# Stage-1 tables in two pieces, smaller first loads of the kernel rows, and an early SiLU table, in a fused long-convolution and MLP kernel

## The chip, the cores and the metric

The kernel runs on one core of a Trainium2 chip. Its time is the device time of one execution in microseconds (us). Eleven executions are known: 180.72 to 186.76, median 183.02. One more was taken with the hardware profiler; it took 181.62, and its trace is the source of every duration below.

The engines: TensorE (PE, with its weight loads, PEld, shown apart), VectorE (DVE), ScalarE (ACT), GpSimd (POOL) and SyncE (SP). SP and POOL issue the DMA transfers here, and ACT issues three small ones at the start.

## The reference

Sequence S = 2048, width D = 640, inner width F = 1728, one batch, bfloat16.

```
xn = layernorm(x)
kv = causal_shift_conv4(k, shift_k) * v
y  = irfft(rfft(pad(kv)) * rfft(pad(ssm_k)))[:S] + kv * ssm_D     # convolution over the sequence
s  = xn * y
g  = silu(gelu(xn @ w1 + b1) @ w2 + b2)
out = x + s * g
```

## The kernel before

**Two halves of work.** The MLP (xn @ w1, gelu, @ w2, silu) is the larger part of TensorE's work. The convolution is done as a two-stage transform written as matmuls with sine and cosine tables. The 640 channels are cut into two blocks b of H = 320 columns; the 2048 tokens lie as 128 partitions by NJ = 16 rows j.

**The convolution's path.** Stage 1 (op kinds `s1k` for the kernel `kT`, `s1u` for the product `kv`; matmuls at L641) multiplies each token row j with the table `W[:, j, :]`. A unit covers 1024 columns in two halves, numbered 2i and 2i+1, so `s1k4` and `s1k5` are one unit. A half is 512 columns of block b's 16 x 320, so `s1k4` reads rows j = 6 and 7, `s1k8` reads j = 12 to 14. Each half takes a pair of the 8 PSUM banks, is evicted by ACT or DVE (`s1ev`, all evictions have line L268) into one of **three staging slots** (two in the tile `mm`, one in the tile `G`), and the unit is stored to DRAM (`s1st`, L646, issued by SP or POOL) as `scrK` or `scrU`. Stage 2 reads the transposed form back (`kin`, `uin`, L750), multiplies (`s2k`, `s2u`, L767), evicts (`s2ev`), forms complex products on DVE (`prod`, `comb`), transforms back (`i1`, L799; it takes two pairs of banks), evicts (`i1ev`) and stores (`cst`, L810, to `scrC`). At the end `cin` (L841) reads it back, `i2` (L821) makes the result and `ym` (L828, DVE) multiplies it into `xn`; `fin` (L555, L561) adds x and `store` writes out. There are 12 conv units (6 for each b). `uin` rotates over four slots, so unit u+4 is loaded after `cst` of unit u has landed.

**The MLP's path.** `xt` transposes xn on PE (L492), `xtev` evicts; `f1h` and `f1` are the first matmuls (L507; `f1h` is half a column group), `f1p` the last rows of two groups (L538), then `gelu` (L513), `f2` (L588), `silu` (L592) and `f2m` (L595, halves at L601).

**The tables.** On DVE `iq0`, `iq1`, `iq2` (L453, L456, L458) make the angles for all 16 rows in one 128x1024 instruction each; two ACT `wsin` (L462, L464) turn them into the sine and cosine halves of `W`. All of `W` is one buffer, so the first stage-1 matmul waits for the second `wsin`. `tabsin` (L443) makes the small stage-2 tables with Silu first, to have the table set that holds both Silu and Sin. `wbm` and `wbev` (L472) spread the shift weights over the partitions, and `kv` units (L664 to L671, DVE) use them. `warm` (L315) are ten matmuls of zeros. `presin` (L306) is one Silu of one element per partition.

**The order.** Ops, dependencies and candidate engines are declared in the code, but the order, the engine of each op and the PSUM and staging slots come from a written table, `ORDER`: each word names the next op, its engine and its slots. Each engine runs its ops in that order; SP and POOL issue DMAs in that order too, so a DMA whose data is late holds the later ones of its queue. In the version before, PE runs all fillers, then `s1k8 s1k4 s1k9`, then the first `f1h`; ACT starts with table load, evictions, table load, `wsin`.

Of the kernel before, what the change touches and what calls it, by code (L numbers as in the profile page):

```python
# [11 lines left out]
I32 = mybir.dt.int32  # L12
# [25 lines left out]
NB = 512  # L38
NS1 = NJ * H // NB // 2
# [98 lines left out]
2d 4p0 7g 5s 1s -19d 20s -5a 46p0 1a -3p1 -9d 1d 4p2 -24d 32p3 -46g 15d 24a -52p4 31d 1d -22g 19g -23p0 -1p2 -2p0 1p2  # L138
44d 8a -23g 16a -41p0 -7p1 52p0 -18a -5d 44p10 -40d -35p2 8p4 43a 26p2 -39d -1d 24a -22d 1g 15d -37s 7s -2s 53a -52s
-5s 1s 58d 103p60 -10p41 -158d 29d -21s 162p0 -81p20 80a 2a -143d 40p3 -2p6 24p7 -23a 6d 86a -90d 3d 19p0 4p 4a -90s  # L140
21g 1d 39d 37p1 1a -15p 10p3 1a 49p42 -82d 46p6 -67s -37s 61d 80a -36a -24p 66p0 -5p4 45d 1d -29s -121s 60p3 -13a 63a
-86g 1d 2d 14p6 70s -50a -11p7 55a 46d -106p 6a -50s 45a 66p00 2p4 -1a -64a 5p3 -28d 4p21 85a -86d -1d 27a -47s 144d
-154d 64p7 -26p6 117d -116d -6a 129d -126p0 -2p1 1d 25p4 96d -91a 98d 1d 1d 1d 7d -6d 7d 1d 1d 1d 7d -147a -25s 87p21
9s -8a -96s 57a 40p6 -35p5 84s 190d -329s -28a 119a 76d -29s 149d -228p00 14p1 -2p4 3a 100d 1d 1d -93p2 1a -17p3 1a
1p1 23s -15p2 -5a -16a 4a 53p62 2p4 -37a 38a -31p3 243d -241a -89s 329d -262p0 -4p2 25a 202d -174a -44a -4a 80p41 2p6
1a -68p3 1a 65a -84p0 1a 43s -32p1 -81s 82a 41g 51p60 1a 1p4 -91p0 -17a 224d -115a -91a 70s 101p10 2p2 -1a 2a -97p62
2p4 1a 17d -204d 316d -110p01 77p31 2p2 32d 1g -295s 176s 8a -2d 3p4 76a -68d -31a 101a 33d -37d -71p00 111d -300s
335d -144p6 74d -78a 231s1 -223d -5a 61p30 -85g 170d -144a 74p21 -78s 232p4 -224d 105a -49a -129p02 130p3 45a -31a
-70d 1d 101a -94d 132g 1d -214a 69s 75p2 -266s -43s 295a 165s0 -220d 7d 49d 166a -296p6 75p01 102s0 1s -101p4 67a -62d
132a -69d 1p30 2p2 32s 131s0 -310a 75a -74s 76a 219p6 4p0 -154a 2a 149a 5p4 9s1 -10a 2a -221d 1d 1d 132a -126d 124d  # L150
-64p31 2p2 -1a 64a -137s 75a 145d1 -296p60 1a 146d -145p0 1a 294d -121s 126d 1d -214d 64p30 151p46 -150a -64d 125s1 3s
88a -151p2 155p0 2p6 -7a -300p42 86d 61d 6p31 153a -305a 86d 7d -95s 90p01 122s 97a 3p4 -157a 159p6 -1a -224d 2d 224a
-159p3 -4a 158d1 -209p00 -9p4 211s -300p6 154a 17p20 16p3 23s 109s1 -220a -9a -89a 171a 136d -217s 222d 1d 1p04 -313s
91d 227s0 17s0 -21a -128a 3p6 -97d 118p70 10p2 -127d 1d 96a -95d 116a 25p3 79d 1g -215p01 120a -118p6 134a -9p2 -124a
-6p4 140a -9a -155p62 28d -26p0 23d 113p3 -135a 259s2 -261d 138a 106p4 2p0 1a -2d 3d1 -144p2 1a 145p6 2p0 -3d 4a -2a
11p4 -164p3 1a 13p2 -109g 260d 15s2 -165a 166s3 -254s 239p0 -10d 14p6 2p4 1d -2a -4a -126p3 18p2 -17a -214p62 2p4
368s1 -41d -225s 128a -229a -2d 353p0 -14d2 15a -122p3 97p64 -326s 328a -1d -97a -5p2 117d 1d 9p0 4p4 2p6 -5a -16d
30s1 -10a -3d0 5a 1d -182p3 1a 150s -112p0 1a -32p1 1a 157p46 1a 10d 6d -135a -13p0 133d -132a 164s0 1s0 -203p1 1a
185p42 1d -144p0 145a -17s -127a 148p6 2p2 10p4 -232d 233d -10a -2a 3d1 -200p1 1a 209p2 4p6 2p4 -200p0 195d 4a 9s2
-23d -266p1 282a -281d 103p6 -22a 176g -153a 186p2 -1s2 -254d 256a -25p40 1a -272p7 1a 272a 8d2 -214p6 220d -5d -219p2  # L160
225d -220a 229p4 4p0 -237a 234d 13s1 -8p6 -1a -184p3 156s 15p40 -170a 12p21 160a 13d 8s3 17s0 1s1 -40a -158a 167d0 6d
8p6 2p0 4p4 -19d 16a -183p3 187d -6d -180a 172d -14s 29p4 10p0 -9a 10a -196p20 181d1 -180a -2d 183d 5d 10p6 14s2 -13a
-27p40 1a 27d2 13s0 -39a -171p2 199p6 2p4 10p0 -9a 42s0 -44d -199a 171s 14d 41s1 -15a 42s1 -246p31 220s2 -15p6 4p4 2p0
-16d 36s2 -230a 195d -194p2 239s3 -247d 212a 6a -2a -20d -11p60 -176a 178a -166p30 165a 2s -166a 205p4 1a -25p06 10d0
1d 5d 1d -15d -343p2 -4p3 371p4 1d 1d1 -221d 222d -28a -345d 4a 358p06 2a -200p2 199a -198a 1d 208p46 2d -1a 9p0 1d
-38s 39p2 10p4 1d -230d 231d -230p61 219d 2p0 5p4 -708a 483a 3d -30p70 223s 30d -5d -9p2 -2p4 12p0 -9d -2d -3g 34s0
-267p6 1a 247d 20p2 4p4 4s1 -277a 257d 13d -243p0 244d -12s2 19p6 4p2 -254a 246d -271d 257p4 -246p00 265d -21s -228d
-14p1 267d 3s3 -271a 260d 9d -12s -255a 247p6 23p2 -26d 1d 1s 30p4 -37s 24d 5s -4s -272p01 2p1 277d -12s -11d 29d 3d
1s -288a 256d 1s 28d 1s -278d 273d -279a 280s -279d 276d 1s
# [3 lines left out]
def kernel(  # L173
# [87 lines left out]
    def eng(e):  # L261
        return nc.vector if e == "DVE" else nc.gpsimd
# [4 lines left out]
    def evict(e, out_, in_):  # L267
        (nc.scalar.copy if e == "ACT" else nc.vector.tensor_copy)(out=out_, in_=in_)  # L268
# [22 lines left out]
    tok_b, m_b, q_b, a_b, W_b, G_b, tab_b = (Buf() for _ in range(7))  # L291
# [5 lines left out]
    m_v = mm[:, 4 * D:4 * D + 2 * 1024].bitcast(I32)  # L297
    a_v = mm[:, 8 * D:8 * D + 2 * 1024].bitcast(I32)
# [7 lines left out]
    op("presin", "ACT", lambda e: nc.scalar.activation(out=acs[:, CH - 1, 0:1], in_=bias_h[:], func=ACT.Silu), reads=[bias_b])  # L306
# [21 lines left out]
    def load(fn, kb, **kw):  # L328
        return op("load", "SP", fn, size=int(kb * 1024), **kw)
# [32 lines left out]
    for b in range(2):  # L362
        for i in range(2):
            load(lambda e, b=b, i=i: nc.sync.dma_start(out=kT[:, b, 8 * i:8 * i + 8, :], in_=kT_v[:, b, 8 * i:8 * i + 8, :]), 640,
                 writes=kT_b[b][8 * i:8 * i + 8], after=firsts[-1:])
# [76 lines left out]
    def tabsin(e):  # L442
# [10 lines left out]
    op("iq0", "DVE", lambda e: eng(e).tensor_tensor(  # L453
        out=m_v.rearrange("p (a b) -> p a b", a=NJ), in0=tok[:, :, None].to_broadcast([P, NJ, N1]),
        in1=k4[:, None, :].to_broadcast([P, NJ, N1]), op=ALU.mult), reads=[tok_b], writes=[m_b])
    op("iq1", "DVE", lambda e: nc.vector.tensor_scalar(out=m_v, in0=m_v, scalar1=19, scalar2=19, op0=ALU.logical_shift_left,  # L456
                                                       op1=ALU.arith_shift_right), writes=[m_b])
    op("iq2", "DVE", lambda e: nc.vector.scalar_tensor_tensor(out=a_v, in0=m_v, scalar=-1.0, in1=m_v, op0=ALU.mult, op1=ALU.min),  # L458
       reads=[m_b], writes=[a_b])
    W_c = W[:].rearrange("p j (k c) -> p c (j k)", c=2)  # L460
    sc = 2.0 * math.pi / L
    op("wsin", "ACT", lambda e: nc.scalar.activation(out=W_c[:, 1, :], in_=m_v, func=ACT.Sin, scale=-sc * (1.0 - EPS)),  # L462
       reads=[m_b, bias_b], mods=[W_b])
    op("wsin", "ACT", lambda e: nc.scalar.activation(out=W_c[:, 0, :], in_=a_v, func=ACT.Sin, scale=sc, bias=bias_h[:]),  # L464
       reads=[a_b, bias_b], mods=[W_b])
    tmp_hold = [m_b, a_b]
# [3 lines left out]
    for i in range(5):  # L470
        ps = bank()
        op("wbm", "PE", lambda e, ps=ps, i=i: nc.tensor.matmul(out=ps.v[:], lhsT=xtra[0:1, 1024:1024 + P], rhs=wrow_f[:, i * 512:(i + 1) * 512],  # L472
                                                              start=True, stop=True), reads=[wr_b, z_b], writes=[ps])
        op("wbev", "ACT|DVE", lambda e, ps=ps, i=i: evict(e, wb_f[:, i * 512:(i + 1) * 512], ps.v[:]), reads=[ps], writes=[wb_b[i]])
# [150 lines left out]
    def s1_unit(src, src_b, scr, scr_b, i, kind, b):  # L625
        o = Buf(pool=stg_pool, parts=2)
        stages.append(o)
        for t in range(2):
            ps = pair()
            base = NB * (2 * i + t)  # L630
            segs, c = [], base
            while c < base + NB:
                z = min(base + NB, (c // H + 1) * H)
                segs.append((c // H, c % H, z - c, c - base))
                c = z

            def mms(e, segs=segs, ps=ps):
                for j, c, n, at in segs:
                    for h in range(2):
                        r = slice(64 * h, 64 * h + 64)  # L640
                        nc.tensor.matmul(out=ps.v[:, h, at:at + n], lhsT=W[r, j, :], rhs=src[r, b, j, c:c + n], start=True, stop=True)  # L641
# [53 lines left out]
    for i in range(CH):  # L695
# [7 lines left out]
        op("gtr", "PE", gtr, reads=[W_b, id_b], writes=[ps], extra=[u for o in stages for u in o.users])  # L703
# [200 lines left out]
```

## Time and profile before

| what | us |
|---|---|
| median of 11 executions | 183.02 |
| the profiled execution | 181.62 |
| its span, first to last instruction | 179.8 |
| outside the span | 1.82 |
| busy: PE, DVE, ACT, POOL | 169.4, 165.2, 147.0, 17.9 |
| first stage-1 matmul starts | 10.79 |
| last instruction of PE ends | 175.20 |

The profiled execution is 1.40 below the median, so a sum made against it is moved by 1.40 to be compared with the median. A busy share is an average over stages. What counts in a stage is which engine has no idle time, and what ended the idle time of the others. A group's mean is the duration of one instruction; consecutive ACT or DVE instructions overlap a little, so the start-to-start distance in the timeline is the better price of one in a row. For PE the distance between starts is the price: a unit of `f1` takes 1.10, `f1h` 0.55, `f2` 2.0, a stage-1 half 0.28, an `s2` 0.26, `i1` 0.54.

### The profile page before, as it was taken

To read this page: it belongs to the slowest core of one execution; us is meant where nothing else is said; L and a number is where in the kernel's file an instruction comes from. 1 tells how busy PE (TensorE), PEld (TensorE's weight loads), DVE (VectorE), ACT (ScalarE), POOL (GpSimd) and SP (SyncE) were. 2 spreads that over 40 slices of the span, in tenths; PEclk is the share of its full clock that TensorE was granted. 3 is DMA by queue.
4 is the path that set the end of the run, shared out by engine and by line. 5 is a ranking of instruction groups with operands and counts; after the bars stand their busy time and mean duration, and the time that the engine had idled before them with its cause. 6 is when DMAs were issued, how large, how long until landed. Compare 5 with 4: busy or idle time off the path is not lost.

```text
span 179.8 us, 4833 instructions
## 1 busy us (share of the span) xinstructions
PE 169.4 (94%) x1971; PEld 93.0 (52%) x1971; DVE 165.2 (92%) x296; ACT 147.0 (82%) x207; POOL 17.9 (10%) x31
## 2 busy tenths in 40 slices
PE   5979999999999999999999999999999999988990
PEld 1346555444566666656444434344465655654660
DVE  7998989999999999998999969999999999966993
ACT  4999999999998989989999999999899998111110
POOL 7440400001004500000002000010000000100000
PEclk9999999999999999999999999999999999999999
DMA  5999999999696899999298997879896999659284
GB/s 141 378 411 410 359 320 319 422 419 411 228 325 232 288 348 175 360 292 246 90 322 225 295 367 243 248 226 302 240 310 204 288 298 342 187 171 401 106 315 178
DMA packets 42025, 51.43 MB, mean 286 GB/s; under 512 B 7170, under 2 KB 31123, under 8 KB 42004
## 3 DMA queue, kind: packets, MB, share of 16 engines
q1 hardware_dynamic: 41104, 48.41, 84.1%
q0 software_dynamic: 752, 2.72, 4.3%
q8 instruction: 15, 0.25, 0.6%
q10 hardware_dynamic: 148, 0.01, 0.1%
q14 instruction: 6, 0.05, 0.1%
HBM read 31.47 MB, written 18.35 MB: 277 GB/s over the span
## 4 chain that ended last, share of the span: by engine, by line
PE 62%; DMA 19%; DVE 9%; ACT 7%; issue 2%; POOLq 0%; DVEq 0%; SPq 0%
PE ps L507 24%; PE ps L588 23%; DMA scrC<-v_all 7%; PE ps L641 6%; DMA scrU<-G 4%; PE ps L767 4%; DMA v_all<-scrU 3%; DVE xn L828 3%; DMA mm<-scrC 3%; PE ps L799 2%; DVE x L555 2%; ACT v_all L268 2%; DVE G L268 1%; DVE kT L555 1%; PE ps L538 1%
## 5 line engine op out<-in xcount | busy, mean ns | idle before, releaser
L588 PE MATMUL ps<-w_sb,hT 128*128 128x320 bf16 x432 | 63.4, 300 | 0.0
L507 PE MATMUL ps<-xnT,w_sb 128*128 128x512 bf16 (+1 forms) x280 | 61.0, 365 | 0.0
L588 PEld LDWEIGHTS <-hT 128*128 128x128 bf16 x448 | 41.9, 98 | 21.2 <-issue 5.7
L507 PEld LDWEIGHTS <-w_sb 128*128 128x128 bf16 x280 | 25.4, 98 | 28.2 <-issue 5.2
L513 ACT ACTIVATE hT<-ps,b_f 128x512 bf16<-128x512 f32 (+1 forms) x56 | 36.8, 697 | 1.5 <-PE ps L507 0.8
L592 ACT ACTIVATE sl<-ps 128x320 bf16<-128x320 f32 x32 | 14.0, 442 | 22.2 <-PE ps L588 16.7
L268 ACT CAST v_all<-ps 128x960 bf16<-128x960 f32 (+2 forms) x35 | 31.1, 911 | 1.1 <-PE ps L799 0.6
L268 ACT CAST mm<-ps 128x1024 bf16<-128x1024 f32 (+1 forms) x27 | 25.0, 957 | 0.3 <-PE ps L472 0.2
L828 DVE TENSOR_TENSOR xn<-ps,xn 128x640 bf16<-128x640 f32 x16 | 12.6, 815 | 2.8 <-PE ps L821 2.8
L268 ACT CAST G<-ps 128x1024 bf16<-128x1024 f32 x12 | 12.2, 1015 | 0.6 <-DMA scrU<-G 0.4
L667 DVE TENSOR_TENSOR mm<-k_all,mm 128x2560 bf16<-128x2560 bf16 x8 | 11.9, 1490 | 0.2
L664 DVE TENSOR_TENSOR mm<-k_all,mm 128x2560 bf16<-128x2560 bf16 x8 | 11.9, 1487 | 0.1
L268 DVE CAST v_all<-ps 128x960 bf16<-128x960 f32 (+2 forms) x11 | 11.5, 1061 | 0.5 <-ACT hT L513 0.3
L767 PEld LDWEIGHTS <-tabs 64*32 64x32 bf16 x704 | 7.6, 90 | 7.0 <-issue 6.0
L268 ACT CAST k_all<-ps 128x960 bf16<-128x960 f32 x11 | 10.6, 961 | 0.8 <-PE ps L767 0.7
L810 POOL DMA_DIRECT2D scrC<-v_all x3 | 2.5, 818 | 86.6 <-DMA scrC<-v_all 34.0
L395 POOL TENSOR_TENSOR rstd<-veps,mhalf 128x4 f32<-128x4 f32 (+2 forms) x6 | 8.6, 1440 | 24.3 <-DVE veps L393 24.3
L641 PEld LDWEIGHTS <-W 64*128 64x128 bf16 x192 | 6.5, 94 | 8.1 <-issue 5.9
L780 DVE TENSOR_TENSOR k_all<-v_all,k_all 128x960 bf16<-128x960 bf16 x16 | 9.7, 649 | 0.0
L780 DVE TENSOR_TENSOR k_all<-v_all,xtra 128x960 bf16<-128x960 bf16 (+1 forms) x16 | 9.1, 608 | 0.2
L767 PE MATMUL ps<-v_all,tabs 64*32 64x240 bf16 (+1 forms) x352 | 8.5, 262 | 0.4 <-DMA v_all<-scrU 0.3
L641 PE MATMUL ps<-kT,W 64*128 64x320 bf16 (+4 forms) x96 | 6.8, 254 | 1.1 <-ACT W L464 0.9
(104 smaller groups left out, 206.2 us busy)
## 6 DMA issues: line engine op xcount, KB each, us to landing
mm<-scrC SPq DMA_DIRECT2D x8, 640.0 KB, 5.6
v_all<-scrU SPq DMA_DIRECT2D x10, 480.0 KB, 4.3
scrU<-mm SPq DMA_DIRECT2D x8, 512.0 KB, 3.4
scrC<-v_all SPq DMA_DIRECT2D x8, 480.0 KB, 4.5
k_all<-scrK SPq DMA_DIRECT2D x7, 480.0 KB, 5.2
kT<-in_kT_dram SPq DMA_DIRECT2D x4, 640.0 KB, 6.3
scrK<-mm SPq DMA_DIRECT2D x5, 512.0 KB, 5.5
v_all<-in_v_dram SPq DMA_DIRECT2D x4, 640.0 KB, 7.6
```

Of the source, the lines that this page charges most:

```text
L268: (nc.scalar.copy if e == "ACT" else nc.vector.tensor_copy)(out=out_, in_=in_)
L395: pows.append(op("pow", "POOL", lambda e: nc.gpsimd.tensor_tensor(out=rstd[:, a:b], in0=veps[:, a:b], in1=mhalf[:, 0:b - a], op=ALU.pow), ...
L507: nc.tensor.matmul(out=ps.v[:, lo * P:hi * P], lhsT=w1_sb[:, ft, t, :], rhs=xnT_b[c].v[:, t, lo * P:hi * P], start=(t == 0), stop=(t == DT ...
L513: op("gelu", "ACT", lambda e: nc.scalar.activation(out=hT_b[c].v[a:z, ft, :], in_=ps.v[a:z, :], func=ACT.Gelu_apprx_tanh, bias=b1_f[a:z, f ...
L588: nc.tensor.matmul(out=ps.v[:, 0:H], lhsT=hT_b[c].v[0:M, ft, q * P:(q + 1) * P], rhs=w[:, h * H:(h + 1) * H], start=(ft == 0), stop=(ft == ...
L592: op("silu", "ACT", lambda e, h=h, ps=ps: nc.scalar.activation(out=sl.v[:, h * H:(h + 1) * H], in_=ps.v[:, 0:H], func=ACT.Silu), reads=[ps ...
L641: nc.tensor.matmul(out=ps.v[:, h, at:at + n], lhsT=W[r, j, :], rhs=src[r, b, j, c:c + n], start=True, stop=True)
L664: op("kv2", "DVE", lambda e: tt(out=kt_t, in0=win(0, 2), in1=wbc(0, 2), op=ALU.mult), reads=kb + [wb_b], writes=[kvt_b], extra=[u for b in ...
L667: op("kv2", "DVE", lambda e: tt(out=kt_t, in0=win(2, 2), in1=wbc(2, 2), op=ALU.mult), reads=kb + [wb_b], writes=[kvt_b])
L767: nc.tensor.matmul(out=ps.v[32 * g:32 * g + 32, r, i * w:(i + 1) * w], lhsT=F2[i][64 * r:64 * r + 64, :], rhs=part(src.v[64 * r:64 * r + 6 ...
L780: nc.vector.tensor_tensor(out=q[:, r], in0=uu[:, r, :, None, :].to_broadcast([P, 2, 2, w]), in1=ku[:, r, None, :, :].to_broadcast([P, 2, 2 ...
L828: nc.vector.tensor_tensor(out=xv, in0=ps.v[:, :, 0:H], in1=xv, op=ALU.mult)
```

## The change

- `W` becomes two buffers: rows 0 to 3 (WJ = 4) and rows 4 to 15. Each has its own `iq0`, `iq1`, `iq2` (128x256 and 128x768) and two `wsin`. A stage-1 op waits only for the piece that its rows are in.
- The angles' scratch places move; the second `a_v` piece uses a part of `mm` past the staging slots.
- The loads of `kT` for b = 0 are three (rows 0 to 4, 4 to 8, 8 to 16) instead of two, and may be issued from the first load on.
- The `wbev` evictions come after `presin`, which so loads the SiLU set before any copy on ACT.
- `ORDER` is a new table: nearly every op has another place, and some have other engines.

```diff
+WJ = 4
...
-    m_v = mm[:, 4 * D:4 * D + 2 * 1024].bitcast(I32)
-    a_v = mm[:, 8 * D:8 * D + 2 * 1024].bitcast(I32)
+    wend = 10 * D + 8 * NB
+    m_v = [mm[:, 4 * D:4 * D + 512].bitcast(I32), mm[:, 4 * D + 512:4 * D + 2048].bitcast(I32)]
+    a_v = [mm[:, wend:wend + 512].bitcast(I32), mm[:, 4 * D + 2048:4 * D + 3584].bitcast(I32)]
...
-    for b in range(2):
-        for i in range(2):
-            load(lambda e, b=b, i=i: nc.sync.dma_start(out=kT[:, b, 8 * i:8 * i + 8, :], in_=kT_v[:, b, 8 * i:8 * i + 8, :]), 640,
-                 writes=kT_b[b][8 * i:8 * i + 8], after=firsts[-1:])
+    for b, a, z in ((0, 0, 4), (0, 4, 8), (0, 8, NJ), (1, 0, 8), (1, 8, NJ)):
+        load(lambda e, b=b, a=a, z=z: nc.sync.dma_start(out=kT[:, b, a:z, :], in_=kT_v[:, b, a:z, :]), 80 * (z - a),
+             writes=kT_b[b][a:z], after=firsts[0:1])
...
+    def wtab(g, j0, j1):
+        m_b, a_b = Buf(), Buf()
+        n = j1 - j0
...
+        op("iq0", "DVE", lambda e: nc.vector.tensor_tensor(
+            out=v3(m_v[g]), in0=tok[:, j0:j1, None].to_broadcast([P, n, N1]),
+            in1=k4[:, None, :].to_broadcast([P, n, N1]), op=ALU.mult), reads=[tok_b], writes=[m_b], size=n)
...
+        op("wsin", "ACT", lambda e: nc.scalar.activation(out=W_c[:, 1, j0:j1], in_=v3(m_v[g]), func=ACT.Sin, scale=-sc * (1.0 - EPS)),
+           reads=[m_b, bias_b], mods=[W_b[g]], size=n)
...
+    wtab(0, 0, WJ)
+    wtab(1, WJ, NJ)
...
-        op("wbev", "ACT|DVE", lambda e, ps=ps, i=i: evict(e, wb_f[:, i * 512:(i + 1) * 512], ps.v[:]), reads=[ps], writes=[wb_b[i]])
+        op("wbev", "ACT|DVE", lambda e, ps=ps, i=i: evict(e, wb_f[:, i * 512:(i + 1) * 512], ps.v[:]), reads=[ps], writes=[wb_b[i]], after=[pres])
...
-            op("s1" + kind, "PE", mms, reads=[src_b[b][g[0]] for g in segs] + [W_b], writes=[ps], hold=[o])
+            op("s1" + kind, "PE", mms, reads=[src_b[b][g[0]] for g in segs] + [W_b[x] for x in sorted({int(g[0] >= WJ) for g in segs})], writes=[ps], hold=[o])
```

What the new `ORDER` says, read as lists (numbers after a colon are the first bank of a pair, or the bank):

```
PE, start, before:  ... xt1 | s1k8:6 s1k4:4 s1k9:0 | f1h0 xt3 xt2 f1h1 f1h2 f1h6 ...
PE, start, after:   ... xt1 | s1k4:6 warm0 s1k5:4 s1k6:0 s1k7:2 wbm2:6 warm2:7 | xt3:4 f1h0:5 xt2:7 s1k8:0 s1k9:2 | f1h1:4 f1h3 f1h7 ...
ACT, start, before: wbev3 wbev0 wbev2 wsin asum wsin wbev4 xtev0 s1evk8 s1evk9 xtev2 s1evk4 gelu2 ...
ACT, start, after:  presin wbev1 wsin wbev3 asum wbev0 wsin xtev0 wbev4 s1evk4 s1evk5 s1evk6 s1evk7 xtev2 s1evk8 s1evk9 wsin wbev2 tabsin wsin gelu0 ...
SP, start, before:  x x x w1a kT8-16 x kT0-8 w1b w1c w1d x k ...
SP, start, after:   x x x kT8-16 kT4-8 w1a x x w1b w1c w1d k kT(b=1) w2a kT0-4 ...
PE, middle, before: s1u12:6 s1u13 f1 s2k4 s2u4 f1 s2k5 s2u5 s2k6 f1 f1 s2u6 s2k7 s2u7 f1 f1 s1k18:6 s1k19 s2k8 f1 i1
PE, middle, after:  s1u17 s1u14 f1 s1u15 s1u18 s1u19 f1 f1 f1 s2k6 s1k18:6 s1k19 f1 i1(banks 2,3 and 6,7)
staging slot of s1k18, before: the one stored last by s1u12/13 (POOL); after: the one stored last by s1u16/17 (POOL)
PE, end, before:    i1 (last unit) i2 i2 i2 f2 i2 i2 f2 i2 i2 i2 f2 | i2 (b=1) ...  f2 f2 of row j = 12 last
PE, end, after:     i1 (last unit) i2 i2 i2 f2 i2 i2 f2 i2 i2 i2 f2 | i2 (b=1) ...  f2 f2 of row j = 15 (stored in halves) last
last cst, before:   POOL; after: SP
```

Over the whole program ACT has 7 table loads after the change and 8 before. ACT evicts two more `xnT`, one more `wb` and one more `s1u`, and has one `s2ev`, one `i1ev` and two `xn` fewer, which go the other way on DVE. POOL issues 7 stores (three of `scrK`, two of `scrU`, two of `scrC`) where it issued 6 (one, two and three). The number of matmuls is the same.

## Prediction, on record before the changed kernel ran

> **What bounds the kernel now.** I read the page's busy times first, then the busy time of each engine in four stretches (start and end, length, then busy us and instructions of PE, PEld, DVE, ACT and POOL, the granted clock, the DMA share, GB/s), the timeline of the first 40 us, and the chain of waits.
>
> ```profile
> PE 169.4 (94%) x1971; PEld 93.0 (52%) x1971; DVE 165.2 (92%) x296; ACT 147.0 (82%) x207; POOL 17.9 (10%) x31
> ```
>
> ```profile
> 0.00:40.00 40.00, 36.80 (x245) 18.28 (x246) 36.19 (x76) 37.29 (x52) 9.52 (x23) 1.00 0.95 353
> 40.00:100.00 60.00, 59.93 (x668) 34.51 (x665) 57.95 (x93) 56.58 (x78) 6.86 (x6) 1.00 0.94 274
> 100.00:152.00 52.00, 50.95 (x882) 26.47 (x868) 49.34 (x92) 48.76 (x68) 0.84 (x1) 1.00 0.92 278
> 152.00:176.00 24.00, 21.74 (x195) 13.69 (x192) 20.86 (x37) 4.41 (x12) 0.71 (x1) 1.00 0.69 241
> ```
>
> In the second and third stretch PE is idle 0.07 and 1.05 us of 112; DVE and ACT are idle 4.7 and 6.7. So PE bounds the program from its first tables to the last conv unit, with two nearly full engines beside it. PE's work is the same after the change, so only three things can move the time: how early PE gets steady work, how long it stands still in the middle, and the tail, where it waits on a DMA and shares the end with DVE. A shorter ACT or DVE counts only where PE waits for it.
>
> **The head.** The timeline has what sets the first stage-1 matmul and what follows it:
>
> ```profile
> 9.32 1.41 ACT L464 ACTIVATE W<-mm,bias_h 128x1024 bf16<-128x1024 int32 x1
> ...
> 10.79 0.78 PE L641 MATMUL ps<-kT,W 64*128 64x64 bf16 x11 [0.89 <-ACT W L464]
> ...
> 11.64 1.94 ACT L268 CAST mm<-ps 128x1024 bf16<-128x1024 f32 x2
> ```
>
> Prices on ACT in a row (start to start): table load 1.30, `wbev` 0.48, the two `wsin` 1.22 and 1.29, `asum` 1.56, `xtev` 0.59, a stage-1 eviction 0.91, a gelu 0.59. A `wsin` of 768 elements I take at three quarters, 0.92 and 0.97; of 256 at 0.4 (both may be more by a fixed part; if all of it were fixed, 0.3 and 0.9 more). ACT's first table load starts at 2.03, when its three DMA issues are done, and still does. ACT after the change: 2.03 + 1.30 + 0.15 (`presin`) = 3.48, `wbev` 3.96, `wsin` 4.9, `wbev` 5.4; x rows 2 and 3 land at 6.0 (issued 1.68, 4.3 to landing), `asum` to 7.55, `wbev` 8.03, `wsin` 9.0. DVE has the angles ready at 6.7 (1.23 + 0.96 + 1.21 times 3/4, with two `stats` between), before they are read. So the first stage-1 matmul goes from 10.79 to 9.0, **1.8 us earlier**.
>
> That gain does not last. After `xtev` and `wbev` (10.07) ACT evicts four halves: 10.98, 11.9, 12.8, 13.7. These four hold all eight banks, and PE's next work takes its banks from them: `s1k9` needs the pair freed at 13.7, and the second `f1h` follows at 14.1. Before, the second `f1h` ran at 13.39. PE is then 0.71 later with three stage-1 halves more behind it, 3 x 0.28 = 0.84. **Net -0.1 us.** From there I follow the same rows on to the second group's `xnT`: its four `xtev` are on ACT now and end at 28.25, PE reaches its reader at 28.5. So PE is fed, with 0.25 to spare; if ACT is late by 1 us, that 1 us is lost, and if ACT runs ahead 1 us earlier at 13.7, up to 0.9 is won. Bounds of the head -0.9 to +0.9.
>
> What is hidden: the split angles add three DVE instructions, 0 to 0.2 each, on an engine that now loses two `xtev` there. The last table piece, its `wsin` and `tabsin` run on ACT at 16.1 to 17.9 and push gelu from 16.4 to 19.3; PE has banks until the first gelus. The last `wbev` ends at 17.5 and `kv` starts at 18.7 (18.90 before), cover 1.2. The piece of `kT` with rows 0 to 4 is loaded behind 6800 KB; by the GB/s row of the page (5.9 MB moved by 18 us, then 320 GB/s) it lands about 22, and `dadd` reads it near 25. Rows 4 to 16 are issued ahead of `w1a`: they landed at 8.42 behind it (2.62 + 5.8), so by about 8.4 with the 320 KB piece, before 9.0.
>
> **The table load that goes** is worth 1.30 of ACT (L443: starts 30.73, next activation 32.02; gelu before it ends 30.71). It buys no PE time, as PE does not wait for ACT there. The Trainium skill (ScalarE: Activation LUTs, What ACT_TABLE_LOAD costs) adds a drain of about 1.38 us to each load, 2.66 in all. This trace shows no gap of that kind on either side of a load. By the page the switch would free 2.66 of ACT, which would still be off PE's path.
>
> **The middle.** Of PE's 1.1 us, the largest piece (0.38) ends this chain:
>
> ```profile
> 95.40 0.78 PE ps L641 x14
> 96.18 0.68 ACT hT L513
> 96.86 0.05 issue
> 96.91 1.22 DVE G L268
> ...
> 98.67 7.77 DMA scrU<-G
> ...
> 107.83 0.61 PE ps L799 x16
> ```
>
> A stage-1 half ends (96.18), is evicted (98.13), POOL stores the unit; the next user of that staging slot (`s1k18`) can be evicted only when the store has landed, and `i1` needs that half's banks. Without the store's 7.77 there are 3.8 us of fixed steps: 1.95 to the end of the eviction, 0.54 to the issue, 0.1 of signals and 1.24 for the next eviction, which ends at 107.80; with it 11.65. PE had 11.27 of work between, so it stood 0.38.
>
> After the change the pattern returns with another unit, again stored by POOL, and with less work between: five `f1` (5.5), four `s1u` and two `s1k` (1.7), one `s2k` (0.26), **7.45 us**. Now ACT evicts (1.0 for 1.24), so the steps are 3.6 plus the landing. POOL's stores landed in 3.4, 4.0, 4.9, 5.1 and 7.8. With 5.1 (same size, and the mean of the five is 5.0) PE waits 3.6 + 5.1 - 7.45 = **1.25 us**; with 3.4 nothing, with 7.8 it waits 3.95. Behind the waiting eviction ACT holds a gelu, `i1ev` and the following `s2ev`, so nothing of PE's refills. The 0.38 goes, as its place has no such user. Net +0.9, from -0.4 to +3.6.
>
> The other 0.7 of idle is left as it is. Its main row is `uin` behind `cst` (0.31 at 126.76, 13.0 us after `i1` of that unit). In the new order the same two are separated by 0.8 less PE work, but a PE that waits 1.25 earlier gives that time back.
>
> **The tail.**
>
> ```profile
> 153.77 3.93 DMA scrC<-v_all
> ...
> 157.75 4.89 DMA mm<-scrC
> ...
> 162.69 0.48 PE ps L821 x4
> ```
>
> PE waits 1.46 for this `cin`, which waits for the last `cst`, issued by POOL. After the change SP issues it; SP's only 160 KB store landed in 2.6, so it is there by 156.3. What is late next is the 480 KB store before it (issued 152.2, 5.1 to landing, 157.3). Gain 157.7 - 157.3 = 0.4. The Trainium skill (DMA: Bandwidth & Descriptors, Latency and other measured facts) gives a first byte at about 1 us from GpSimd and 0.6 from SP. By that page alone the move is worth 0.4 on the transfer, by the rows 1.3 and 0.5 of issue; the other store limits both to 0.4.
>
> PE's work after it is equal (five `f2`, eight `i2`). Ending with halves of row 15 leaves 1.1 us behind the last matmul (silu 0.44, `f2mh` 0.3, `fin` 0.33) for 1.69 now, but DVE's list there is as long as before (plus 0.1) and was full, so I take 0.2 of the 0.6. Tail -0.6, from -1.0 to +0.2.
>
> **Sum.** -0.1 + 0.9 - 0.6 = +0.2: 181.62 becomes 181.8, and with the 1.40 to the median **183.2**. All good ends give -0.9 - 0.4 - 1.0 = -2.3, 180.7; all bad ends +4.7, 187.7.
>
> **Rivals.**
> - *PE is fed throughout.* POOL's store lands in 3.4 to 4.0 and ACT stays ahead at the head: -0.4 in the middle, -0.6 in the tail, -0.5 in the head: -1.5, **181.5**. For it: ACT has 1.3 us less table work and is the engine that frees the banks. Against: the stage-1 halves still leave through ACT one by one.
> - *The staging slot becomes the bound.* The store lands in 7.8 as in the chain above, since `kin` and `uin` loads of 480 KB fill the queues at this point in both orders (DMA share 0.99 there): +3.6 - 0.6 - 0.1 = +2.9, **185.9**. It is slower by more than 0.5% from a landing time of 5.9 on.
> - *The split does not start the tables earlier*: the first stage-1 matmul stays at 10.8 because the pieces' fixed costs eat the split. Then the four evictions come 1.8 later, and so does PE at the second `f1h`: 0.2 + 1.8 = +2.0, 185.0. The `wsin` rows speak against it; I fold it into the slower case.
>
> **Chances.** My forecast 0.42 (183.2, from 182.1 to 184.6; three quarters of it within 0.5% of 183.02, a quarter above), PE fed 0.30, slot or late tables 0.28. 0.5%, 0.9 us, is about what a measurement of this kernel tells from no change. Faster 0.30, same 0.31, slower 0.39. The range leaves out the best tenth and the worst tenth: 180.7 to 186.2.
>
> **What would show it.** First stage-1 matmul near 9.0, second `f1h` not before 13.9; seven table loads; PE idle before an `i1` near 103 to 106, released by an ACT eviction that waited for `scrU`; last `cst` from SP with `cin` issued about 5.1 after the 480 KB store. The prediction is wrong if PE shows idle between 14 and 60, or none at that `i1`, or if the tail after the last conv unit is longer than 27.5 us (152.3 to 179.8 now).

## The result: 1.1% slower, and the profile after

The changed kernel takes 184.87 us (median of 12 executions, 183.16 to 189.56); the kernel before, measured beside it, 182.8 (47 executions). The ratio is **1.0114, 95% interval 1.0073 to 1.0156**, some 2 us. The profiled execution took 183.16, the shortest of the twelve and 1.7 below their median, with a span of 181.4 (181.62 and 179.8 before). In some executions TensorE's granted clock falls to 0.50 for 3 to 4 us (the last section shows when); lengths across such a stretch are compared below only where the text says so.

The same two views as before, first the busy times, then the four stretches:

```profile
PE 171.6 (95%) x1971; PEld 93.3 (51%) x1971; DVE 165.4 (91%) x299; ACT 145.0 (80%) x208; POOL 17.5 (10%) x32
```

```profile
0.00:40.00 40.00, 38.10 (x244) 18.73 (x245) 35.35 (x76) 36.22 (x55) 10.36 (x24) 1.00 0.97 375
40.00:100.00 60.00, 59.17 (x645) 34.09 (x643) 58.28 (x97) 56.18 (x75) 4.79 (x5) 1.00 0.92 266
100.00:152.00 52.00, 49.24 (x857) 24.65 (x856) 47.32 (x86) 45.66 (x65) 2.39 (x3) 1.00 0.84 255
152.00:176.00 24.00, 23.93 (x224) 15.22 (x223) 21.88 (x38) 6.53 (x14) 0.00 (x0) 1.00 0.74 254
```

PE is busier at both ends (38.10 for 36.80 in the first stretch, 23.93 for 21.74 in the last) and idler in the middle: 0.83 + 2.76 us, where it was 0.07 + 1.05. So the start and the end look better and the middle worse.

| us | before | after |
|---|---|---|
| first stage-1 matmul | 10.79 | 8.89 |
| second `f1h` (start of its row) | 13.23 | 14.44 |
| first `i1` | 77.20 | 79.12 |
| last `i1` | 152.23 | 155.69 |
| last `i1` to the end of the span | 27.6 | 25.7 |

**Head**, from the timeline:

```profile
7.69 1.15 ACT L475 ACTIVATE W<-mm,bias_h 128x768 bf16<-128x768 int32 x1
8.89 0.61 PE L655 MATMUL ps<-kT,W 64*128 64x192 bf16 x4 [0.60 <-ACT W L475]
9.27 4.24 ACT L270 CAST mm<-ps 128x512 bf16<-128x512 f32 x5
```

The last sine ends 1.9 us earlier and PE starts with it. Then ACT evicts one `wbev` and four stage-1 halves in a row, to 13.51, and the second `f1h` waits for their banks until 14.44.

**Middle**, from the chain of waits (start, duration, what):

```profile
96.13 0.40 PE ps L655 x4
...
96.56 1.24 DVE mm L270
...
98.32 6.77 DMA scrU<-mm
...
105.19 1.02 ACT mm L270
...
106.25 0.60 PE ps L813 x14
```

It is the pattern that the prediction showed for another unit: a half ends, is evicted, POOL's store takes 6.77, and only then can `s1k18` be evicted into the same staging slot and `i1` have its bank. PE's idle before 106.25 is 1.84. The other idle is three `uin` loads that PE waits for: 0.83 at 71.29, 0.47 at 133.65 and 0.45 at 139.80.

**Tail**, from the timeline, and the last 480 KB store from the list of DMA issues:

```profile
156.74 0.36 SPq L824 DMA_DIRECT2D scrC<-v_all  x1
159.78 3.84 SPq L855 DMA_DIRECT2D mm<-scrC  x4
...
164.62 0.73 PE L835 MATMUL ps<-mm,G 128*64 128x320 bf16 x8
```

```profile
scrC<-v_all SPq DMA_DIRECT2D x1, 480.0 KB, 4.0
```

The first `i2` of the second block has no wait in front of it now (1.46 before): the 480 KB store took 4.0 to landing instead of 5.1, and `cin` went out 4.1 us after the last `i1` instead of 5.5.

### The profile page after: what moved, and what is told of

Its sections match the earlier page's. It is cut to its first block, busy times and chain, and to the rows that moved or that the text cites. A ratio compares the mean times of both kernels' runs of the same rounds, so it can differ in the third digit from the quotient of the medians.

```text
span 181.4 us, 4838 instructions
## 1 busy us (share of the span) xinstructions
PE 171.6 (95%) x1971; PEld 93.3 (51%) x1971; DVE 165.4 (91%) x299; ACT 145.0 (80%) x208; POOL 17.5 (10%) x32
## 4 chain that ended last, share of the span: by engine, by line
PE 71%; DMA 13%; DVE 8%; ACT 4%; issue 1%; SPq 1%; ACTq 0%; DVEq 0%; POOLq 0%
PE ps L521 27%; PE ps L602 25%; DMA v_all<-scrU 7%; PE ps L655 5%; PE ps L781 5%; DMA scrU<-mm 4%; DVE xn L842 3%; PE ps L813 3%; DMA x<-in_x_dram 2%; PE ps L835 2%; DVE x L569 2%; PE ps L552 1%; DVE kT L569 1%; PE ps L506 1%; ACT v_all L270 1%
## 5 line engine op out<-in xcount | busy, mean ns | idle before, releaser
L270 ACT CAST mm<-ps 128x1024 bf16<-128x1024 f32 (+1 forms) x30 | 27.5, 948 | 3.1 <-DMA scrU<-mm 2.4
L270 ACT CAST v_all<-ps 128x960 bf16<-128x960 f32 (+2 forms) x32 | 28.2, 909 | 2.0 <-PE ps L781 1.1
L270 DVE CAST v_all<-ps 128x960 bf16<-128x960 f32 (+2 forms) x14 | 15.1, 1082 | 2.9 <-PE ps L781 1.8
L270 ACT CAST k_all<-ps 128x960 bf16<-128x960 f32 x12 | 11.5, 965 | 1.2 <-PE ps L781 0.9
L397 POOL TENSOR_TENSOR rstd<-veps,mhalf 128x4 f32<-128x4 f32 (+2 forms) x6 | 7.4, 1235 | 40.0 <-DVE veps L395 40.0
L270 ACT CAST G<-ps 128x1024 bf16<-128x1024 f32 x11 | 11.2, 1029 | 0.0
L609 DVE TENSOR_TENSOR xn<-xn,sl 128x640 bf16<-128x640 bf16 x14 | 6.8, 485 | 1.3 <-ACT sl L606 1.2
```

The source lines that it names most:

```text
L397: pows.append(op("pow", "POOL", lambda e: nc.gpsimd.tensor_tensor(out=rstd[:, a:b], in0=veps[:, a:b], in1=mhalf[:, 0:b - a], op=ALU.pow), ...
```

## Experiments

**Theory after the result.** Head about level; the staging slot behind a POOL store costs the middle 1.84, with late `uin` loads beside it; the last `cst` on SP gave back 1.5 in the tail. **Rivals:** the edits themselves cost (new small instructions, tables in front of the first gelu); a stall that is removed comes back at the next wait; the tail's gain has nothing to do with the queue of the last store.

### 1. The store that the slot waits for, on SP

```diff
- POOL: ... s1stk7 s1stu8 s1stu9 ...
- SP:   ... uin3 kin4 uin4 ...
+ POOL: ... s1stk7 s1stu9 ...
+ SP:   ... uin3 kin4 s1stu8 uin4 ...
```

> The kernel after, with one DMA moved: the store of the unit s1u16/17, whose staging slot s1k18 takes next, is issued by SP (behind kin4) instead of POOL; nothing else changes. Theory (the slot's store makes PE wait): the store is issued near 97.8 instead of 98.3 and lands in about 5.4 (the median of SP's stores of scrU in the run after) instead of 6.8, so the evictions of s1k18/19 start near 103.3 instead of 105.2, and PE's 1.84 of idle before that i1 is at most 0.3. The profiled time falls by 1.5 to 1.8, from 183.2 to 181.4-181.7. Rival (the queues are full there, whoever issues): it lands in 6.3 or more, over 1.0 of the idle stays, 182.3 or more. Second rival (another wait takes its place): the idle goes but comes back before s2u or the next i1, less than 0.7 gained.

SP's timeline, ACT's, and the list of DMA issues:

```profile
98.52 0.53 SPq L660 DMA_DIRECT2D scrU<-mm  x1
```

```profile
104.10 1.01 ACT L270 CAST mm<-ps 128x1024 bf16<-128x1024 f32 x1 [0.68 <-DMA scrU<-mm]
```

```profile
scrU<-mm SPq DMA_DIRECT2D x1, 512.0 KB, 5.5
```

The eviction ended at 98.45; SP issued 0.07 later. In experiment 3, on the same chip with the store on POOL, the eviction ended at 99.02, the issue came 0.53 later and the landing took 6.6. Together 1.56 us, and **PE's wait there is gone**. From first to last `i1` it takes 74.71 instead of 76.57. The ratio to the kernel before is 1.0005 (0.9888 to 1.0121), an interval that also holds the 1.0114 of the kernel after. The theory holds for this wait; the first rival expected a landing of 6.3 or more. The profiled time did not follow: 185.59 where 181.4 to 181.7 was expected. The second `f1h` came only at 15.94 there, PE waited 0.89 for a `uin` at 127.72 and 2.01 for `cin`, and a stretch at half clock follows the 2.01. So the second rival, another wait, has its part.

The Trainium skill (DMA: Bandwidth & Descriptors, Latency and other measured facts) gives a first byte 0.4 us earlier from a hardware queue than from GpSimd's. The two runs here differ by 0.46 in the issue and by 1.1 in the landing, more than the page's figure.

### 2. The two halves later, POOL still storing

```diff
- PE: ... s2k6 s1k18 s1k19 f1 i1 f1 s2u6 s2k7 s2u7 f1 f1 f1 s2k8 ...
+ PE: ... s2k6 f1 i1 f1 s2u6 s2k7 s2u7 f1 f1 f1 s1k18 s1k19 s2k8 ...
```

> The kernel after, with the two halves s1k18 and s1k19 and their evictions put about 5 us of PE work later (behind the i1 that waited, three f1 and three s2), POOL still storing the unit ahead of them. Theory (too little PE work between the two users of the slot): the store has landed before the halves' evictions come, whoever issued it; the 1.84 before i1 is gone, PE idle from 100 to 152 falls from 2.8 to about 1.0, profiled time 181.3 to 181.7. Rival (the halves are needed early): kin6, the first load of the second block, needs their store; it goes from 113.4 to about 116 or later, and PE waits at the first s2k of the second block, so that 1.0 or more of the gain is lost: 182.4 or more.

The wait before that `i1` went (0.15 left), and the kernel became slower: 1.0432 (1.0112 to 1.0751, from 4 executions). The waits of SP's queue and of PE (who waited for whom: us in total, times, longest):

```profile
SPq L660 <- DVE mm L270: 12.2, 1, 12.2
```

```profile
PE ps L781 <- DMA k_all<-scrK: 2.1, 1, 2.1
```

SP comes to the store of these halves in its old place and stands there for 12.2 us, with a `cst`, a `uin` and `kin6` behind it. PE then waits 2.08 for `kin6`, and 0.89 for ACT before. The rival holds: the halves may not be late, and a queue in order passes the delay on to loads that have nothing to do with it.

### 3. and 4. The last `cst`: on POOL in the kernel after, on SP in the kernel before

```diff
- after:  SP ... cst10 cst11 cin ...     before: POOL ... cst11
+ after:  POOL ... cst11                 before: SP ... cst10 cst11 cin ...
```

> The kernel after, with the last cst issued by POOL as in the kernel before. Theory (the tail's gain is the last store's queue): PE's wait before the first i2 of the second block is back at 1.0 to 1.5, the tail after the last i1 grows from 25.7 to 26.7-27.2, profiled time 184.2 to 184.7. The prediction's own account (the 480 KB store ahead limits both): 0.4 longer, 183.6. Rival (the tail is shorter by the end in halves and the order of f2): 0.2 or less, 183.2 to 183.4.

> The kernel before, with only its last cst issued by SP instead of POOL. Theory (queue alone): the wait of 1.46 before the first i2 of the second block falls to 0.3 or less, and the time by 1.0 to 1.4: 180.2 to 180.6 against 181.6 in the profiled execution. The prediction's own account: 0.4, 181.2. Rival (the new order of PE's end is needed for it): less than 0.2.

In 3, PE waited 2.38 before the first `i2` of the second block, more than the 1.0 to 1.5 that the theory asked (median 186.23 of 4 executions, 183.74 for the kernel before beside it). But in 4, where the wait should have gone, it grew from 1.46 to 1.90:

```profile
163.37 0.73 PE L821 MATMUL ps<-mm,G 128*64 128x320 bf16 x8 [1.90 <-DMA mm<-scrC]
```

The ratio is 1.0004 (0.9939 to 1.0069). **My theory of the tail falls.** In 4 the last 480 KB store landed in 5.9, in 3 in 6.5; the last 160 KB store comes in half a us behind it from either queue. `cin` went out 6.55 after the last `i1` with the store on POOL and 6.30 in experiment 1 with it on SP. The queue is worth no more than that 0.25, and perhaps less, since the 480 KB store itself landed in 6.2 there for 6.5. The prediction's own account had 0.4.

### 5. The kernel after, once more

> The kernel after, unchanged: a second profile of it, to see which of its differences stay. Theory (the middle's stall is a property of the order, the shorter tail a draw of how fast the last stores land): from the first i1 (79.1) to the last (155.7) again 76.6, within 0.3, with 1.6 to 1.9 of idle before the third unit's i1; behind the last i1 the 480 KB store lands in 5 to 6.5 instead of 4.0, PE waits 1 to 2.4 for cin before the first i2 of the second block, and the tail is 27 to 28.3 instead of 25.7. Rival (the tail's 1.9 is the last store's queue and the new end): 25.5 to 26.0 again, no wait before that i2.

ACT's timeline at the staging slot:

```profile
104.52 1.01 ACT L270 CAST mm<-ps 128x1024 bf16<-128x1024 f32 x1 [2.30 <-DMA scrU<-mm]
```

From first to last `i1` 76.01, with 1.71 of idle before the same `i1`, and no wait for `uin` over 0.15. The last 480 KB store took 7.4, and PE waited 2.82 for `cin`. The tail was 30.7, beyond the expected 27 to 28.3, as a stretch at half clock follows that wait. Ratio 1.0068 (0.9966 to 1.0170). The stall in the middle belongs to the order; the good tail of the first profile does not.

### 6. All edits of the code, with the order of before

```diff
- ACT: wbev3 wbev0 wbev2 wsin   asum wsin   wbev4 xtev0 ... s1evk4 gelu2 ...
+ ACT: presin wbev3 wbev0 wbev2 wsin(large) asum wsin(large) wbev4 xtev0 ... s1evk4 wsin(small) tabsin wsin(small) gelu2 ...
```

> All edits of the code (table in two pieces, three loads of the first kernel block, SiLU first), with the order of the kernel before: each new op stands beside its sister, the small piece's two wsin and tabsin behind the fifth stage-1 eviction, before the first gelu. Theory (the loss is the new order's, not the edits'): the first stage-1 matmul goes from 10.79 to 9.1-9.9, the first i1 from 77.2 to 76.2-77.2, nothing changes behind it, and the time is 0 to 1.0 below the kernel before (ratio 0.995 to 1.000). Rival (the edits cost: three more DVE and two more ACT instructions, tables in front of the first gelu): first i1 at 77.7 or later, ratio 1.004 or more. Rival (the split's 1.8 reaches PE): first i1 at 75.8 or earlier, ratio below 0.993.

The first stage-1 matmul came at 9.04, but the first `i1` at 78.92, and the ratio is 1.0102 (1.0044 to 1.0161). PE's timeline has the reason:

```profile
17.51 0.39 PE L654 MATMUL ps<-kT,W 64*128 64x256 bf16 x4 [0.55 <-ACT W L474]
...
21.57 0.40 PE L654 MATMUL ps<-kT,W 64*128 64x64 bf16 x6 [1.10 <-ACT G L269]
```

This order wants a row of the small piece (`s1k2`) before ACT has made it, and the first evictions and gelus are pushed back by it. So the edits do cost when the order does not know of them. The theory's 0 to 1.0 of gain was not there. It is one placement of mine, not the best one, so it is no proof that the edits can't gain under the old order.

### 7. The small piece's tables made ahead of the first stage-1 matmul

```diff
- ACT: ... wbev0 wsin(large) xtev0 ... s1evk9 wsin(small) wbev2 tabsin wsin(small) ...
- DVE: ... iq2(large) xn xn ... iq0 xtev1 ... iq1 ... iq2(small) ...
+ ACT: ... wbev0 wsin(small) wsin(small) wsin(large) xtev0 ... s1evk9 wbev2 tabsin ...
+ DVE: ... iq2(large) iq0 iq1 iq2(small) xn xn ...
```

> The kernel after, with the small piece's angles and its two wsin moved ahead of the last wsin of the large piece, so that the first stage-1 matmul stands behind the whole table as before. Theory (ACT is one chain there; the split only reorders it): the first stage-1 matmul 0.8 to 1.1 later (9.7 to 10.0, or at the landing of the kernel rows if these come later), the second f1h 0.3 to 1.0 later, but the first gelu no more than 0.2 later since the two wsin are gone in front of it; the first i1 within 0.4 of the unchanged kernel in the same company. Rival (the early start is worth its 0.9): first i1 0.7 to 1.1 later.

First stage-1 matmul 9.72 (8.91 in experiment 5, on the same chip), second `f1h` 15.72 (14.78), first `i1` 79.47 (78.44): **0.81, 0.94 and 1.03 later**, as the rival asks. Ratio 1.0187 (1.0116 to 1.0257). But one pair of profiles doesn't show it. In seven profiles with the head of the new order unchanged, the second `f1h` lies anywhere from 13.89 to 16.52 and the first `i1` from 77.90 to 80.36, later the later TensorE reaches its full rate (table in the last section). Full rate came at 14.86 here; beside the unchanged head nearest to that (experiment 2, 15.07) the second `f1h` is 0.04 earlier and the first `i1` 0.14 later. So neither the theory nor the rival is shown.

### 8. Two stores of the kernel before on SP

```diff
- POOL: ... cst1 s1stu6 cst4 cst11
+ POOL: ... cst1 cst4          (s1stu6 ahead of s1stu8 on SP, cst11 behind cst10)
```

> The kernel before, with two stores issued by SP instead of POOL: the one of s1u12/13, whose staging slot s1k18 takes next (0.38 of PE idle in its profile, 0.87 in the run with the last cst on SP), and the last cst. Theory (a store that somebody waits for is 1.0 to 1.5 earlier on SP): the idle before the third unit's i1 is gone, first to last i1 from 75.0-75.3 to 74.5, and the time falls by 0.4 to 0.9 in the middle and 0 to 0.3 in the tail, ratio 0.993 to 0.998. Rival (PE is bound by its own work and another wait takes its place): within 0.2 of the kernel before.

The wait before the third unit's `i1` (0.38 before, 0.87 in experiment 4) is gone; first to last `i1` takes 74.76. Ratio 0.9952 (0.9899 to 1.0004): as the theory has it, though the interval just touches no change.

### 9. A copy ahead of the SiLU table

```diff
- ACT: presin wbev1 wsin(large) ...
+ ACT: wbev1 presin wsin(large) ...      (and wbev no longer behind presin)
```

> The kernel after, with one wbev ahead of presin on ScalarE (and no order between wbev and presin), so that the first table load is for a copy and the SiLU set is loaded behind it: eight table loads instead of seven. By the rows of the kernel after, the first sine then starts 1.3 to 1.5 later, the last sine ends near 9.9 instead of 8.9. The prediction's account (the load that goes buys no PE time): first i1 within 0.3 of the unchanged kernel (78.4 to 79.1). Theory after the run with the table in one piece (what comes ahead of the first stage-1 matmul on ScalarE moves everything behind it one for one): first stage-1 matmul 9.7 to 10.1, first i1 0.7 to 1.2 later, 79.3 to 80.2.

ACT's timeline and PE's:

```profile
2.02 1.28 ACT L270 ACT_TABLE_LOAD   x1 [2.02 <-issue]
...
3.92 1.28 ACT L309 ACT_TABLE_LOAD   x1
```

```profile
9.95 0.61 PE L655 MATMUL ps<-kT,W 64*128 64x192 bf16 x4 [1.66 <-ACT W L475]
```

Each load takes 1.28, and the second one now stands in the chain of the first table: the last sine ends at 9.90, for 8.56 in experiment 5. The first stage-1 matmul moves less, from 8.91 to 9.95, because in experiment 5 it waited for `kT` and not for the table. The second `f1h` is at 16.13, the first `i1` at 79.87 (78.44 and 79.12 in the two profiles of the kernel after), the ratio 1.0175 (1.0077 to 1.0274). Full rate came at 15.47 here; the unchanged heads on either side of that (experiments 2 and 11, 15.07 and 15.76) have their first `i1` at 79.33 and 79.67. So the early SiLU is worth 1.34 us at the last sine and, by these two, 0.2 to 0.5 at the first `i1`; the prediction's account (within 0.3) and the theory (0.7 to 1.2) are not told apart. By the Trainium skill (ScalarE: Activation LUTs, What ACT_TABLE_LOAD costs), which adds a drain of about 1.38 us, the load would move what stands behind it by up to 2.66; the last sine moved by 1.34, about the 1.28 of the load itself.

### 10. to 12. The `cin` loads of the first block ahead of `uin11`

After experiment 5 the question was what sets the landing of the last stores. On SP three `cin` of 640 KB stand behind `uin11`, which waits until POOL's `cst7` has landed.

```diff
- SP: ... kin11 cin3 uin11 cin1 cin2 cin0 cst8 ...
+ SP: ... kin11 cin3 cin0 cin1 cin2 uin11 cst8 ...
```

10 is this alone, 11 adds the edit of experiment 1, and 12 is the kernel of experiment 8 with its `cin` moved in the same way.

> The kernel after, with the three 640 KB cin loads of the first block moved ahead of uin11 on SP's queue; uin11 waits for the store of the unit whose slot it takes (POOL's cst, 4.9 to 7.2 to landing), and the loads behind it with it. Theory (the length of the tail is the distance between these loads and the last stores: uin11 issued 11.3 us ahead of the last i1 and a last 480 KB store that lands in 4.0 in the profile after; 8.6 to 10.5 us and 6.2 to 7.0 in the runs with a PE wait of 2 to 2.8): the three loads are issued near 140 to 143, the last 480 KB store lands in 3.9 to 5.0, PE's wait before the first i2 of the second block is at most 0.5, the tail behind the last i1 is 25.5 to 26.5, and the median of the time lies 0.5 to 1.5 below that of the kernel after (ratio to before 1.003 to 1.009 instead of 1.011). Rival (the stores' landing is set by the chip and the execution): the wait is 1 to 2.8 again, ratio 1.009 to 1.014.

> The kernel after with both changes: the store of s1u16/17 issued by SP, and the three cin loads ahead of uin11. Theory: first to last i1 74.7 instead of 76.6, tail 25.5 to 26.5, ratio to before 0.988 to 0.997. Rival (DVE and PE's own work bound both versions, the waits only move): ratio 0.998 to 1.005.

> The kernel before with the stores of s1u12/13 and the last cst issued by SP, and two cin loads ahead of uin11. Theory: the gain of the two stores alone was 0.5 per cent (ratio 0.995); with the loads out of the last stores' way PE's wait before the first i2 of the second block (1.0 to 1.9) falls below 0.5 and another 0.3 to 1.0 us goes: ratio 0.989 to 0.994. Rival (the end of DVE's list is the bound there): ratio 0.995 to 0.998.

In all three the last 480 KB store landed in 3.0 and PE's wait for `cin` was gone. The tail behind the last `i1` was 25.7, 25.6 and 26.1 (in 10 and 11 a stretch at half clock lies ahead of the last `i1`, not in the tail). Yet the ratios are 1.0079 (1.0024 to 1.0134), 1.0023 (0.9968 to 1.0078) and 0.9995 (0.9947 to 1.0043). SP's and PE's timelines of 10:

```profile
137.26 4.92 SPq L855 DMA_DIRECT2D mm<-scrC  x4
145.50 0.36 SPq L764 DMA_DIRECT2D v_all<-scrU  x1
```

```profile
151.62 0.45 PE L781 MATMUL ps<-v_all,tabs 64*32 64x160 bf16 x16 [2.67 <-DMA v_all<-scrU]
```

The issue of `uin11`, from the list of DMA issues:

```profile
v_all<-scrU SPq DMA_DIRECT2D x1, 160.0 KB, 6.1
```

POOL's `cst7`, issued at 138.12 beside the four loads, takes 7.3 (4.8 in the first profile of the kernel after, but 7.1 in experiment 5 too), and `uin11` behind them takes 6.1 (3.3 in the first profile), so **PE waits 2.67 for it instead** (2.40 in 11, 2.07 in 12). The mechanism holds, and the gain goes to a new wait. Experiment 11 is better than the kernel after in its middle (no wait at the third `i1`), but none of the three beats the kernel before beyond its interval, nor does 1; experiment 8 comes nearest.

The tails of ten profiles put side by side (us; the wait is PE's for `cin`, added up where there were two, and the tail is from the last `i1` to the end). Experiments 1 and 5 are left out, as half clock lies in their tails, and 11 and 12, which repeat the first row with 25.6 and 26.1:

| kernel | last 480 KB store lands in | wait | tail | tail less wait |
|---|---|---|---|---|
| cin early (10) | 3.0 | 0 | 25.7 | 25.7 |
| edits alone (6) | 3.5 | 0 | 26.0 | 26.0 |
| **after** | 4.0 | 0 | 25.7 | 25.7 |
| tables together (7) | 4.8 | 0.82 | 26.5 | 25.7 |
| before, two stores on SP (8) | 4.9 | 1.38 | 27.3 | 25.9 |
| **before** | 5.1 | 1.46 | 27.6 | 26.1 |
| before, last cst on SP (4) | 5.9 | 2.08 | 28.1 | 26.0 |
| copy first (9) | 6.2 | 2.08 | 27.9 | 25.8 |
| after, last cst on POOL (3) | 6.5 | 2.55 | 28.1 | 25.6 |
| halves later (2) | 7.0 | 2.66 | 28.5 | 25.9 |

The wait follows the moment at which this store lands, counted from the last `i1`, and not the queue of the last store. The order has a part in that moment: the new one issues the store 0.50 ahead of the last `i1` (155.19 for 155.69), the old one 0.04 ahead (152.19 for 152.23). That is why a landing of 4.8 gave 0.82 of wait in experiment 7 and one of 4.9 gave 1.38 in experiment 8. Less the wait, the new order's end is shorter by about 0.3.

## Why the prediction was right or wrong

Its range held the time and its likeliest case was too low by 1.7 us: it gave no change, and the kernel is slower. By its own steps, in the profiled execution:

| step | predicted | profile | over the runs |
|---|---|---|---|
| head | -0.1 | +0.4 | second `f1h` from 13.9 to 16.5 in seven profiles |
| idle in the middle | +0.9 | +2.5 | wait at the `i1` 1.6 to 2.2 in six profiles |
| tail | -0.6 | -1.9 | -0.3, and a wait of 0 to 2.8 |
| sum | +0.2 | +1.0 of a measured +1.5 | ratio 1.0114 |

- **Head: mechanism right in the first profile, size off over the runs.** The first stage-1 matmul was due at 9.0 and came at 8.89, the second `f1h` at 14.1 and came at 14.44. Less the three halves more that are done by then (0.84), PE is 14.44 - 13.23 - 0.84 = 0.4 behind. (The prediction read 13.39 for the 13.23; its own sum would have given 0.0.) But this profile was a good draw. Over the seven with this head the median of the second `f1h` is 15.76, which by the same sum is 1.7 behind and outside the stated -0.9 to +0.9. The first `i1` is at 79.33 in the median of the seven and at 77.4 in the four profiles with the old head; by an estimate from the prices of the profile before, 0.6 of that is work done earlier (four `s2` more at 0.26 each, and 8 stage-1 matmuls fewer). The prediction had no term for the half rate at which TensorE starts: its prices are those of later rows. That the new order itself brings full rate later isn't shown, as one order had it at 8.34 and at 17.11. The landing of `kT`, due by 8.4, ended PE's wait for the first stage-1 matmul in four of the seven (8.90 to 9.87).
- **"The table load that goes ... buys no PE time"** is not refuted. The load beside `tabsin` at 30.73 hides, and the one for the gelu behind it (33.49) went with it. The one at 5.25, ahead of the first sine, stood in the head's chain: by experiment 9 one there costs 1.34 at the last sine, and at the first `i1` 0.2 to 0.5 as far as profiles with about the same start tell. Two loads came instead, at 49.49 and 55.19. The prediction had the effect of the one at 5.25 inside the 1.8 of the head, without naming it.
- **The staging slot: mechanism, place and sign right, size off.** "Landing 5.1 ... PE waits 1.25" was 6.77 and 1.84. The slot came back in every profile of the order with POOL's store (1.84, 1.71, 1.65, 1.73, 1.61, 2.18) and in neither with SP's. The choice of 5.1, the mean of POOL's stores, was the mis-sized term; the one row from this very place (7.8) was nearer. That the wait came out within 0.6 is in part luck: with 6.77 the sum would have given 2.9, but the fixed steps took 2.9 instead of 3.6 and PE had 7.9 of work between instead of 7.45.
- **"The other 0.7 of idle is left as it is" failed.** `uin` waits were 1.75 in the profile, against 0.31. They are not steady (0 in experiment 5, 1.32 in 3; under the old order 0.31, 0 in 4, and 1.36 in 6), so much of it may be how fast a `cst` and a `uin` land in that execution. PE's wait earlier on did not give the time back, as the prediction had it. No run isolates how much of it is the 0.8 less work between.
- **Tail: the account was right, its profile misleads.** The 480 KB store does limit `cin`, the queue of the last `cst` is worth 0.25 at most, the halves at the end about 0.3 (0.2 predicted). Of the rest of the 1.9, 0.5 is that the new order issues that store earlier, which the prediction did not have, and 1.1 is a store that landed in 4.0 instead of 5.1 in that one execution. My first reading after the result, that the queue had won 1.5, was wrong.
- **Missing: what a wait costs beyond its length.** In the profile after, no stretch at half clock followed the 1.84, in experiment 7 one did (last section). It is not isolated how much of the medians' 2.1 us it makes. Of the profile's own +1.5, 0.5 stays unplaced. How the 2.1 us of the medians divide between the head and the slot isn't shown either: no run changes the order of the head alone.

Of the rivals, the one of the staging slot came nearest in what happened: not by a landing of 7.8 alone, but by 6.77 and the late `uin` loads together. By its number the one of the late tables (185.0) lies nearest to 184.87, and that is luck: its condition, a first stage-1 matmul at 10.8, did not come. PE was not fed throughout.

## What to carry to other kernels

An order that frees an engine early is worth nothing if the buffer that it needs next comes free by a DMA: write down for each staging slot who stores it, on which queue, and how much work lies until the next user, and take the landing from the row at that place, not from a mean. Count a wait of PE at its length, and 1.7 us besides where 2 us of it can fall into one interval of the clock (next section). A load moved ahead of another on a full queue only moves the wait. Before a gain or a loss at the start or the end is put down to an edit, take more profiles: here the same head reached the second `f1h` at 13.89 and at 16.52, and one DMA's landing went from 3.0 to 7.4 us, and the wait behind it with it.

## What the runs showed of the hardware

**A PE wait of 1.6 us or more can cost another 1.7 us.** In experiment 7 PE waits 1.73 at the staging slot, and then the granted clock (the third number from the right in these stretches) drops:

```profile
106.48 0.60 PE L813 MATMUL ps<-k_all,tabs 32*64 32x480 bf16 x14 [1.73 <-ACT mm L270]
```

```profile
106.00:107.00 1.00, 0.52 (x14) 0.15 (x13) 0.66 (x1) 1.00 (x2) 0.00 (x0) 1.00 0.02 8
107.00:108.00 1.00, 1.00 (x9) 0.43 (x4) 0.76 (x1) 0.85 (x2) 0.00 (x0) 0.51 0.06 25
108.00:109.00 1.00, 1.00 (x4) 0.15 (x1) 0.40 (x1) 0.13 (x1) 0.00 (x0) 0.50 0.99 389
109.00:110.00 1.00, 1.00 (x33) 0.64 (x40) 0.00 (x0) 0.06 (x1) 0.00 (x0) 0.50 0.96 289
110.00:111.00 1.00, 0.84 (x34) 0.40 (x14) 0.31 (x1) 1.00 (x2) 0.00 (x0) 0.79 1.00 276
```

The clock is lost for 0.49 + 0.50 + 0.50 + 0.21 = 1.7 us, and the next unit's `i1` comes 10.85 after this one instead of 9.25. In the fourteen profiles there are 18 waits of 1.6 to 2.8 us; six were followed, within 0.1 to 1.2 us, by such a stretch, always 3.4 us at half clock. No shorter wait was, and no stretch came without a wait, but for the end, where PE has nothing left to do. Six in eighteen times 1.7 makes 0.6 us on top of each such wait; the new order has two places for one (the slot, `cin`), the old order one.

Which of them are followed is more than a draw. In every trace the clock's records change on a grid of 3.41 us (in experiment 7 at 14.86, 107.02 and 110.43, 27 intervals and one apart), and what tells the waits apart is how much idle time lies in one interval. Once full rate was reached, the four intervals with 2.0 us or more were all followed by half clock, of the five with 1.66 to 1.77 two were, and none with 1.61 or less. The wait of 2.01 in experiment 1 lay whole between 163.34 and 166.75 and was followed; the one of 2.39 in experiment 2 was cut by the grid into 1.74 and 0.65 and was not.

The Trainium skill (TensorE: Matmul & The Clock Gate, What's actually happening) has the array fall back to half rate after an idle window of about 3.4 us; here waits of half that length were enough, and the stretch has the window's length.

**TensorE runs the first microseconds at half rate, and how long differs.** The granted clock doesn't show it; it reads 1.00 there. The same 14 stage-1 matmuls in two profiles of the same order, the kernel after and experiment 10:

```profile
9.97 1.46 PE L655 MATMUL ps<-kT,W 64*128 64x320 bf16 x14
```

```profile
9.55 0.96 PE L655 MATMUL ps<-kT,W 64*128 64x320 bf16 x14
```

In each of the fourteen traces the distance between starts halves at one moment (0.21 to 0.11 for a matmul of 256 columns, 0.11 to 0.06 for one of 128), and the trace's clock records begin at that moment. For the head of the new order, the last two rows with their own edits:

| profile | full rate from | first stage-1 | second `f1h` | first `i1` |
|---|---|---|---|---|
| 10 | 8.34 | 8.90 | 13.89 | 77.90 |
| after | 13.10 | 8.89 | 14.44 | 79.12 (0.83 of it a wait for `uin`) |
| 5 | 13.77 | 8.91 | 14.78 | 78.44 |
| 2 | 15.07 | 9.61 | 15.76 | 79.33 |
| 11 | 15.76 | 9.10 | 15.76 | 79.67 |
| 1 | 16.56 | 9.29 | 15.94 | 79.79 |
| 3 | 17.11 | 9.87 | 16.52 | 80.36 |
| 7 | 14.86 | 9.72 | 15.72 | 79.47 |
| 9 | 15.47 | 9.95 | 16.13 | 79.87 |

With the old head it was 9.45, 12.05 and 12.96 (before, 4 and 8), with the first `i1` at 77.20, 77.16 and 77.53; in experiment 12 it was 7.60, but half clock came back from 11.02 to 14.43, and the first `i1` was at 78.39. So the earlier a start is, the more of it falls into the slow part, which a price from a later row doesn't show. The same section of the page says that the array starts at half rate, until it has been busy through one of these windows, which run free of the kernel's start. In the kernel after PE is at work from 1.25 on with one gap of 0.6, and 13.10 is later than that window suggests; why it came so late no run here shows.

**A change of the kind of matmul costs PE about 0.1 us.** In the timeline of the kernel after, `s2` halves in a row start 0.20 to 0.22 apart (127.52, 127.74, 127.94), and an `f1` behind one starts 0.32 later (128.26); the same step appears between `f1` and stage-1 halves and around `i1`. By these rows an order with more such changes would be slower with no idle shown; no run here changes only that.
